# Sigmoid attention with a token and channel mixer: channel products in seven-product form, cast loads, DMA transposes and a fixed order on every engine

## Chip, cores, metric

One core of one Trainium2 chip. The metric is device time in microseconds (us), the median of several executions; a run's time is 1.7 to 1.9 us more than its own span. A run is called slow here when it is over 1.5% above the fastest of its kernel. Medians are of all runs, ratios of the fast ones alone. Engines: PE is the TensorE matmul, DVE VectorE, ACT ScalarE, POOL GpSimd, SP SyncE (which here only issues DMAs). The granted clock is the share of its full clock at which TensorE was let run. A bank is a piece of PSUM, the memory into which TensorE writes its sums.

## The reference, cut to what matters

```python
scores = q @ k.T / 8 - log(448)                  # 8 batches, 12 heads, 448 x 64
x = concat_heads(sigmoid(scores) @ v)            # [8, 448, 768]
u = x + (relu(x.T @ w_tok1) @ w_tok2).T          # token mixer, 448 -> 256 -> 448
out = u + relu(u @ w_ch1) @ w_ch2                # channel mixer, 768 -> 1536 -> 768
```

All tensors are float32; inside, products are float16 with float32 sums.

## The kernel before

Two batches form a group; there are four groups. A group has six head pairs, each with seven score tiles (`scores`), one set of value products and a turn back, then token products (`tok1`, `tok2`), turns of the sums (`uturn`) and the two channel products (`ch1`, `ch2`). The attention of group g+1 is interleaved with the products of group g, over everything but `tok1`. A visit is two score tiles, one behind the other. The order is fixed by hand on TensorE only; a scheduler arranges the other engines. Cut to what the argument touches:

```python
def turn(i):                                  # k and q turned by TensorE, 7 + 7 transposes
    for what in ("k", "q"):
        ps = bank(...)
        for j in range(J):
            nc.tensor.transpose(out=ps[:, j, :, :], in_=src[:, j, :, :], identity=ident)
        nc.vector.tensor_copy(out=kt_or_qt, in_=ps)

def ch1(cb, j0, j1):                          # first channel product, directly
    for db in range(NDB):                     # 6 matmuls into one bank
        nc.tensor.matmul(out=ps, lhsT=w_ch1_t[:, db, 128*cb:128*cb+128], rhs=uT[:, db, j0:j1, :], ...)
    nc.vector.tensor_scalar(out=h2aT[:, cb, j0:j1, :], in0=ps, scalar1=0.0, op0=MAX)

def ch2(j, half):                             # second: 12 matmuls, then one addition and a store
    ...
with tc.manual_schedule(engines={mybir.EngineType.PE}):
    for f in attention_atoms(0): f()          # first group: nothing to interleave with
    for g in range(NG):
        for f in front: f()                   # tok1
        weave(attention_atoms(g + 1), rest)   # tok2, uturn, ch1, ch2 with attention of g+1
```

## Time and profile before

| what | before |
|---|---|
| time | 438.31 us (437.31 to 440.04, 3 runs) |
| span of the profile (of an execution at a granted clock of 0.994), TensorE busy | 432.8 us, 396.2 us |
| first token product of groups 0, 1, 2, 3 starts at | 67.6, 164.8, 262.0, 359.1 us |
| one period: length, TensorE idle | 97.2, 0.8 us |

A period is the time from one group's first token product to the next group's. As TensorE idles for 0.8 us of it, work taken off TensorE ought to come out of the time as long as nothing else takes TensorE's place. The page and the windows behind this are shown in the prediction.

### The profile page before, as it was taken

How to read it: one execution, taken by the hardware profiler on the slowest of the kernel's cores; microseconds unless marked ns; L12 is line 12 of the kernel's file. 1: busy time of each engine (PE TensorE's matmuls, PEld its weight loads, DVE VectorE, ACT ScalarE, POOL GpSimd, SP SyncE). 2: the span in 40 equal slices, each digit the busy share in tenths (PEclk: the TensorE clock that was granted, in tenths of full speed). 3: DMA queues.
4: the chain of work that ended last, by engine and by line, in shares of the span. 5: the costliest groups of instructions: out<-in, count | busy, mean ns of one | idle time of the engine just before them, and what ended most of it. 6: DMA issues, size and time to landing. Idle time of an engine off the chain costs nothing.

```text
span 432.8 us, 8713 instructions
## 1 busy us (share of the span) xinstructions
PE 396.2 (92%) x3712; PEld 215.7 (50%) x3712; DVE 174.8 (40%) x312; ACT 216.8 (50%) x277; POOL 74.5 (17%) x105
## 2 busy tenths in 40 slices
PE   1775668999999999999999999999999999999995
PEld 1343335444555555444565555444555555546663
DVE  2131213845542224844542224844542224855322
ACT  1768884774546643775546643765546643300000
POOL 3851516021221211021221211011000000000000
PEclk9999989999999999999999999999999999999999
DMA  8999999335237643234337643200002221000234
GB/s 202 246 261 248 259 266 216 85 87 108 60 69 180 161 92 69 77 88 105 67 63 180 163 93 73 71 2 2 2 2 74 73 74 38 2 0 2 54 94 109
DMA packets 28023, 44.51 MB, mean 103 GB/s; under 512 B 3280, under 2 KB 23504, under 8 KB 27984
## 3 DMA queue, kind: packets, MB, share of 16 engines
q1 hardware_dynamic: 18304, 33.04, 28.6%
q0 software_dynamic: 9680, 10.92, 15.4%
q8 instruction: 29, 0.48, 0.5%
q14 instruction: 10, 0.08, 0.1%
HBM read 43.84 MB, written 11.01 MB: 127 GB/s over the span
## 4 chain that ended last, share of the span: by engine, by line
PE 85%; ACT 7%; issue 3%; DVE 2%; DMA 1%; SPq 0%; ACTq 0%; DVEq 0%
DMA rawq_0_76<-in_q_dram 1%; PE xa_5_0_787 L168 1%; PE xa_0_0_273 L168 1%; PE c_2_5_1_4890 L286 0%; PE c_2_4_1_4846 L286 0%; PE c_2_4_0_4809 L286 0%; PE c_2_3_1_4746 L286 0%; PE c_2_2_0_4654 L286 0%; PE c_2_1_1_4615 L286 0%; PE c_2_0_0_4490 L286 0%; PE c_1_6_0_3556 L286 0%; PE c_1_5_1_3507 L286 0%; PE c_1_4_1_3463 L286 0%; PE c_1_4_0_3426 L286 0%; PE c_1_3_1_3363 L286 0%
## 5 line engine op out<-in xcount | busy, mean ns | idle before, releaser
L267 PEld LDWEIGHTS <-w_ch_t 128*128 128x128 f16 x576 | 53.4, 98 | 53.8 <-issue 9.7
L286 PEld LDWEIGHTS <-h2aT_4980 128*128 128x128 f16 x168 | 16.4, 98 | 10.9
L286 PEld LDWEIGHTS <-h2aT_3597 128*128 128x128 f16 x168 | 15.6, 98 | 12.5 <-issue 3.2
L286 PEld LDWEIGHTS <-h2aT_2214 128*128 128x128 f16 x168 | 15.6, 98 | 12.5 <-issue 3.2
L286 PEld LDWEIGHTS <-h2aT_831 128*128 128x128 f16 x168 | 15.6, 98 | 12.5 <-issue 3.2
L240 PEld LDWEIGHTS <-w_tok_n 128*64 128x64 f16 x224 | 12.1, 108 | 9.0 <-issue 4.8
L222 PEld LDWEIGHTS <-w_tok_t 64*128 64x128 f16 x224 | 10.6, 94 | 7.8 <-issue 1.0
L131 PE MATMUL tk_0_165<-ident,k_0_74 128*128 128x128 f16 x7 | 0.9, 311 | 7.3 <-DVE k_0_74 L83 7.3
L154 ACT ACTIVATE attn_0_0_184<-qk_0_0_183,att_bias 128x896 f16<-128x896 f32 x1 | 1.0, 1007 | 10.1 <-PE qk_0_0_183 L147 10.1
L131 PEld LDWEIGHTS <-k_0_74 128*128 128x128 f16 x7 | 0.7, 141 | 7.3 <-DVE k_0_74 L83 7.3
L99 DVE COPY w_tok_n<-w_tok_s 128x896 f16<-128x896 f16 x1 | 1.6, 1562 | 5.5 <-DMA w_tok_s<-in_moe_w_tok_dram 5.5
L147 PEld LDWEIGHTS <-kT_0_163 64*64 64x64 f16 x28 | 1.1, 129 | 4.7 <-issue 4.5
L190 DVE COPY x_nat_162<-xb_5_820 128x896 f16<-128x896 f16 x1 | 0.6, 625 | 6.6 <-PE xb_5_820 L187 6.6
L83 DVE CAST k_0_74<-rawk_0_71 128x896 f16<-128x896 f32 x1 | 1.1, 1086 | 5.3 <-DMA rawk_0_71<-in_k_dram 5.3
L83 POOL CAST k_5_3738<-rawk_5_3735 128x896 f16<-128x896 f32 x1 | 0.9, 933 | 12.4 <-issue 12.4
L147 PEld LDWEIGHTS <-kT_2_329 64*64 64x64 f16 x28 | 0.9, 104 | 4.3 <-issue 3.5
L83 POOL CAST k_4_3725<-rawk_4_3722 128x896 f16<-128x896 f32 x1 | 0.9, 934 | 12.4 <-issue 12.4
L83 POOL CAST k_4_959<-rawk_4_956 128x896 f16<-128x896 f32 x1 | 0.9, 933 | 12.4 <-issue 12.4
L83 POOL CAST k_4_2342<-rawk_4_2339 128x896 f16<-128x896 f32 x1 | 0.9, 933 | 12.4 <-issue 12.4
L135 DVE COPY kT_1_225<-tk_1_227 128x896 f16<-128x896 f16 x1 | 0.6, 624 | 5.9 <-PE tk_1_227 L131 5.9
L147 PEld LDWEIGHTS <-kT_5_669 64*64 64x64 f16 x28 | 0.9, 106 | 4.3 <-issue 3.3
L75 POOL DMA_DIRECT2D v_3_953<-in_v_dram x2 | 1.2, 593 | 10.2 <-DMA w_ch_t<-in_moe_w_ch_dram 10.2
(1646 smaller groups left out, 1126.6 us busy)
## 6 DMA issues: line engine op xcount, KB each, us to landing
w_ch_t<-in_moe_w_ch_dram POOLq DMA_DIRECT2D x2, 2304.0 KB, 29.3
rawk_0_71<-in_k_dram SPq DMA_DIRECT2D x2, 224.0 KB, 4.0
rawq_0_76<-in_q_dram SPq DMA_DIRECT2D x2, 224.0 KB, 5.6
rawk_1_89<-in_k_dram SPq DMA_DIRECT2D x2, 224.0 KB, 7.3
rawq_1_94<-in_q_dram SPq DMA_DIRECT2D x2, 224.0 KB, 7.8
rawk_2_102<-in_k_dram SPq DMA_DIRECT2D x2, 224.0 KB, 7.1
rawq_2_107<-in_q_dram SPq DMA_DIRECT2D x2, 224.0 KB, 6.3
rawk_3_119<-in_k_dram SPq DMA_DIRECT2D x2, 224.0 KB, 7.2
```

Source lines behind the costliest of these rows:

```text
L75: eng.dma_start(out=t[64 * b : 64 * b + 64, :, :, :], in_=src[2 * g + b, 2 * i : 2 * i + 2].rearrange("h (p j) e -> p h j e", j=J),)
L83: eng.tensor_copy(out=t[:, :, :, :], in_=raw.rearrange("p h j e -> p j h e"))
L99: nc.vector.tensor_copy(out=w_tok2_n[:, :, :, :], in_=w_tok2_s.rearrange("t c (p j) -> t c j p", j=J),)
L131: nc.tensor.transpose(out=ps[:, j, :, :], in_=src[:, j, :, :], identity=ident[:, :])
L135: nc.vector.tensor_copy(out=kt[:, :, :, :], in_=ps[:, :, :, :])
L147: nc.tensor.matmul(out=ps[64 * b : 64 * b + 64, h, 0:S], lhsT=kT[i][64 * h : 64 * h + 64, j, b, :], rhs=qT[i][64 * h : 64 * h + 64, b, :, ...
L154: nc.scalar.activation(out=at[:, :, :], in_=ps[:, :, 0:S], func=SIGMOID, bias=bias_t[:, :], scale=att_scale,)
L168: nc.tensor.matmul(out=ps[b][64 * h : 64 * h + 64, :], lhsT=vf[64 * b : 64 * b + 64, h, j, :], rhs=attn[(i, j)][64 * b : 64 * b + 64, h, : ...
L222: nc.tensor.matmul(out=ps[b][:, :], lhsT=w_tok1_t[64 * b : 64 * b + 64, j, 128 * tcb : 128 * tcb + 128], rhs=x_nat[64 * b : 64 * b + 64, j ...
L240: nc.tensor.matmul(out=ps[64 * b : 64 * b + 64, :], lhsT=w_tok2_n[:, tcb, j, :], rhs=h1T[:, b, tcb, c], start=(tcb == 0), stop=(tcb == 1),)
L267: nc.tensor.matmul(out=ps[:, :, :], lhsT=w_ch1_t[:, db, 128 * cb : 128 * cb + 128], rhs=uT[:, db, j0:j1, :], start=(db == 0), stop=(db == ...
L286: nc.tensor.matmul(out=ps[:, :], lhsT=h2aT[:, cb, j, :], rhs=w_ch2_t[:, cb, c], start=(cb == 0), stop=(cb == NCB - 1),)
```

## The change

Its intent is to take work off TensorE. The seven-product form (Strassen's) cuts each matrix into four blocks and makes the product from seven products of blocks instead of eight, with sums of blocks before and after. The diff has over 900 lines; its core:

```diff
-with tc.manual_schedule(engines={mybir.EngineType.PE}):
+with tc.manual_schedule(engines=None):              # written order on every engine
-    eng = nc.gpsimd if what == "v" else nc.sync      # k, q raw on SP, rearranged and cast by POOL
+    nc.gpsimd.dma_start(out=t16, in_=src)            # k, q, v: cast loads, all on the Pool queue
 # k and q of groups 1 to 3
-    nc.tensor.transpose(...) x 14; nc.vector.tensor_copy x 2
+    nc.vector.tensor_copy(out=m, in_=raws...)        # rearranged on DVE, one buffer each
+    nc.sync.dma_start_transpose(out=t, in_=m)        # in the visit that starts the head before
 # sums of groups 1 to 3
-    nc.tensor.transpose x 6; nc.scalar.activation(COPY)
+    nc.sync.dma_start_transpose(out=uT[:, :, j], in_=u16)
 # ch1 and ch2: Strassen's seven products of half size instead of eight
+    row_sums(...)                                    # 4 DVE sums of the left matrix, per part
+    piece(1): mm(x, A1, W1); save x                  # x accumulates on: 1, then 6, 7, 4
+    piece(2): mm(y, A2, W2); out11 = clamp(y + saved)
+    piece(6): mm(x, ...); save x ... piece(7), (4), (5), (3)
+    ch2 order of a block: for p in (1, 2, 6, 5, 7, 4, 3): piece(p); add it to u (and twice where needed)
 # interleaving: attention of g+1 lies over ch1(g) and two of three ch2 blocks only;
 # then tok1(g+1), third block, tok2(g+1) with its turns, odd block of g
-    weave(attention_atoms(g + 1), rest)
+    weave(ch1 + blocks[0] + blocks[1], attention(g + 1)); tok1; blocks[2]; tok2; last
 # PSUM: scores, values and turns back share two pairs of banks
 # first group: two value steps behind each score, value copies on DVE
```

I call the stretch in which scores are interleaved with products the **woven stretch**, and what follows up to the next group's first channel product the **token part**.

## The prediction

> **What bounds the kernel now.** I read the page's busy table and slices first, then a stretch by windows, then the chain that ended last, then the timeline of one stretch.
>
> The page of the kernel before (busy us and share, then 40 slices in tenths):
>
> ```profile
> span 432.8 us, 8713 instructions
> PE 396.2 (92%) x3712; PEld 215.7 (50%) x3712; DVE 174.8 (40%) x312; ACT 216.8 (50%) x277; POOL 74.5 (17%) x105
> PE   1775668999999999999999999999999999999995
> ACT  1768884774546643775546643765546643300000
> ```
>
> PE is full from slice 8 on; only the first 70 us are not PE's. One period in the middle, by windows (PE, PEld, DVE, ACT, POOL busy, clock, DMA share):
>
> ```profile
> 167.00:264.00 97.00, 96.17 (x930) 51.92 (x928) 42.47 (x77) 53.76 (x70) 18.02 (x24) 1.00 0.43 100
> ```
>
> The token products of the four groups start at 67.6, 164.8, 262.0 and 359.1, so a period is 97.2 us, and PE is idle for 0.8 us of it. The chain of waits agrees:
>
> ```profile
> PE 85%; ACT 7%; issue 3%; DVE 2%; DMA 1%; SPq 0%; ACTq 0%; DVEq 0%
> ```
>
> The timeline gives the prices that I use:
>
> ```profile
> 83.60 1.00 ACT L154 ACTIVATE attn_0_2_1163<-qk_0_2_1162,att_bias 128x896 f16<-128x896 f32 x1
> 84.49 1.01 ACT L154 ACTIVATE attn_0_3_1170<-qk_0_3_1169,att_bias 128x896 f16<-128x896 f32 x1
> ...
> 90.51 0.36 PE L147 MATMUL qk_1_0_1257<-qT_1_1207,kT_1_1206 64*64 64x448 f16 x4
> 90.80 0.51 PE L257 MATMUL ut_6_1264<-ident,u_0_6_1152 128*128 128x128 f16 x6
> 91.15 1.46 PE L267 MATMUL c_0_4_0_1272<-uT_830,w_ch_t 128*128 128x512 f16 x6
> 92.44 1.46 PE L267 MATMUL c_0_5_0_1280<-uT_830,w_ch_t 128*128 128x512 f16 x6
> 92.65 0.69 DVE L274 TENSOR_SCALAR h2aT_831<-c_0_4_0_1272 128x512 f16<-128x512 f32 x1 [1.55 <-PE c_0_4_0_1272 L267]
> ```
>
> Sigmoids follow each other every 0.89 us although each lasts 1.0. Six matmuls of 512 take 1.29 us, 0.216 each. Four score matmuls of 64x64 run side by side and cost 0.19. Score to transpose takes 0.29, so a change of the array's tiling costs 0.1. DVE starts 0.2 us after the last matmul has been issued.
>
> **What the Trainium skill says.** "TensorE: Matmul & The Clock Gate", Back-to-back issue gap: N/2.4 + 2.5 ns. The trace agrees: 0.216 us for 512, and 1.95 us for twelve of 384, 0.1625 each; so 0.189 for 448. "TensorEngine Tiling (Array Packing)", Key Properties: a change of tiling mode drains the engine; the trace puts it at the 0.1 us above. "VectorE: DVE Perf Modes", the perf-mode tier table: a 16-bit tensor_tensor in SBUF reaches 2x, anything from PSUM in fp32 1x. The trace agrees for PSUM (692 ns for 512 elements is 533 at 0.96 GHz plus 159); it has no 16-bit sum, so I estimate 768/2/0.96 + 159 = 0.56 us. The same page, The three transpose paths, gives 1309 ns for a 128x128 transpose by DMA; the trace has no transposing DMA, and this is my least certain number.
>
> **The change, part by part, for one middle period.**
>
> PE before: k and q turns 84 x 0.056 = 4.7; scores 42 x 0.19 = 8.0; values 6 x 1.33 = 8.0; turns back 42 x 0.056 = 2.4; token products 4.6 and 4.6; sum turns 42 x 0.056 = 2.4; first channel product 12 x (6 x 0.216 + 6 x 0.163) = 27.3; second 14 x 12 x 0.163 = 27.4. Sum 89.4; the 7.8 to 97.2 are some 55 changes of tiling and the idle 0.8.
>
> PE after: seven products for eight. First channel product 7 x 6 x 3 x 0.189 = 23.8 (-3.5). Second: 7 x 3 x 6 x 0.1625 = 20.5, and the odd seventh token block directly 24 x 0.1625 = 3.9, together 24.4 (-3.0). The turns of k, q (-4.7) and of the sums (-2.4) go to the DMA queues. Sum 75.8, with some 54 changes of tiling 81.3. If PE stayed the bound a period would fall from 97.2 to about 82.
>
> DVE has to pay: 42.5 before. Added are 18 add-and-clamp operations and 6 copies of 448 (estimate 448/0.96 + 159 = 0.63 each), 23 instead of 14 additions of 384 (0.555, of which 0.09 overlaps the next), 4 x (0.56 + 0.46) sums of rows for the first product, 12 x 0.56 for the second, 12 rearrangements of k and q (about 0.5) and 6 copies of 896 from PSUM (1.09). The 24 clamps (0.69, 0.56) and the copies of turned k and q fall out. It comes to about 62 us net of overlap. ACT has 42 x 0.895 = 37.6, 8 clamps and 12 saves of 0.43. Neither exceeds 82.
>
> But the three now wait for each other. I walked the written order, which is now fixed on every engine.
> - Attention woven into the channel products: PE work 23.8 + 13.7 (two of three blocks) + 18.4 + 5.4 of tiling changes = 61.3. Scores come in twos with two PSUM pairs. Often one product piece of 0.57 lies between two visits: 0.38 + 0.2 + 0.57 = 1.15 of PE for 1.79 of ACT, a stall of 0.6, with a save on ACT 1.0. In one place two visits are adjacent (2.0). Values and turns back now take one of the same two pairs (0.4 to 0.6 each). An addition must leave PSUM before the next product accumulates there: 0.2 + 0.555 + 0.06 = 0.8 between the last two pieces of a block. Charged in full, this is 14 us, stretch 75. I take half of it, since a wait on PE lets ACT and DVE catch up: 68.
> - Token part, no attention: token product 4.7, third block 6.85 + 0.8, then DVE alone sets the pace: the trace of the last group has one token row block every 1.40 us (two additions, one cast), 9.8, plus 2.4 for sums put before the last. Then the last DMA transpose, and only then the next product. 4.7 + 7.7 + 12.7 + about 2 = 27, though PE has work for 20.
> A period: 68 + 27 = 95, hardly below 97.2. The gain of 16 us of PE work goes to waits.
>
> Start: before, the first product stage begins at 67.6. ACT ran 42 sigmoids and 12 copies in 54 us with gaps; after, the copies are DVE's and score and value steps alternate, so 12.3 + 42 x 0.895 = 50, and two more for the last values: 52. Loads: the trace took 26 MB from HBM in its first 76 us, 0.34 MB/us; what is needed by then (14.4 MB) has come by about 47, also as cast loads. That is 15 us gained. The first token part then waits for DVE: 1.6 + 5.4 for weight sums (four of 2304 elements, 1.35), 1 rearranging, 9.8 + 2.4: first channel product at about 73.5, against 83.3.
>
> End: 23.8 + 20.5 + 3.9 = 48.2 of products without attention, stalls before each block (its sums 2.4 and the first addition before the third piece, 1.8) and inside (0.8) about 8, last store 4: 60. Before: 59.5 from the first channel product.
>
> Sum: 73.5 + 3 x 95 + 2 (sums of the second weights in the first period) + 60 = 420.5. Time minus span was 5.5 before: **426**.
>
> **Rivals.**
> 1. PE stays the bound: waits overlap far better than I walked. Periods of 86: 73.5 + 258 + 2 + 58 + 5.5 = 397. For it: mean shares of ACT (about 50 of 86) and DVE (62) leave room. Against: fixed order, two score buffers.
> 2. All stalls count in full: periods of 103, time 450. For it: before, single waits for ACT in the first 60 us cost PE 1.0 each, and the stall sizes are sums of measured durations. Against: the interleaving seems chosen with care.
> 3. The transposes by DMA are the bound. Only two free buffers hold the cast sums, so the third cast waits for the first transpose; at 4 us each the token part is paced by 2.3 instead of 1.4 and gains 6 us a period; time 445 to 470. Against: 1.3 us for 128x128, and six or seven blocks of one transfer should overlap.
> 4. First loads late on the single Pool queue: 3 to 8 us once. Against: the first cast from the Pool queue (v) landed in 4.2 us before.
>
> **Range and chances.** The sum of parts is 139 + 3 periods + 5.5 within 5 us; the period is what I do not know: 86 to 104. That gives 402 to 457; I take 400 to 456. A gain over 2% needs less than 429.5, a period below 96. The walk alone would say slower, the sums of work say much faster; I lean a little to faster: 0.53, same 0.20, slower 0.27.
>
> **What would show it.** Right: token products of the groups start about 95 apart, PE busy below 85% of the span, about 325 us; first token product near 52; in the woven stretch PE waits for sigmoids and DVE additions; in the token part DVE is over 90% busy and PE under 75%. Wrong: PE above 90% busy (rival 1), waits of sums or of turned k and q for a DMA (rival 3), or a first part above 60 us (rival 4). Matmul pitches other than 0.189 and 0.1625, or an add-and-clamp far from 0.63, would break the sums themselves.

## The result, and the profile after

The kernel after took **495.3 us** (494.83 to 496.85, 4 runs) against 437.81 for the kernel before in the same rounds, a ratio of 1.1355 (95% interval 1.1283 to 1.1427). Ratios here are the mean time of one kernel's fast runs over that of the other's of the same rounds, so not quite the ratio of the medians. The prediction said 426 and gave slower a chance of 0.27.

The page of the kernel after (as before: busy us and share, then tenths in 40 slices; PEclk is the granted TensorE clock):

```profile
span 493.4 us, 7956 instructions
...
PE 386.2 (78%) x3190; PEld 188.6 (38%) x3190; DVE 288.9 (59%) x500; ACT 203.4 (41%) x256; POOL 90.2 (18%) x155
...
PE   3767776786979887488888887778888886799775
...
ACT  2798637364655300646655220445756320022000
...
PEclk9998998797999997979999997779999999799999
```

From slice 8 on, where TensorE was full before, it is 0.4 to 0.9 busy, no other engine is near full, and the clock drops to 0.7 in several slices. That is a kernel bound by waits. By stages (windows of the profile after: length, busy us of PE, PEld, DVE, ACT, POOL, granted clock, DMA share, GB/s), the second woven stretch, the token part after it, and the end:

```profile
199.14:281.48 82.34, 66.90 (x581) 30.25 (x582) 47.32 (x79) 44.43 (x54) 21.43 (x36) 0.96 0.74 99
281.48:314.14 32.66, 25.00 (x187) 14.29 (x187) 20.07 (x40) 5.39 (x10) 0.00 (x0) 0.90 0.46 94
427.91:493.40 65.49, 51.51 (x276) 26.78 (x276) 38.45 (x69) 6.52 (x12) 0.00 (x0) 1.00 0.18 49
```

| stage | predicted | measured |
|---|---|---|
| start to first token product | 52 | 58.2 |
| to the first channel product | 21.5 | 20.5 |
| woven stretches, three | 68 each, and 2 once: 206 | 87.9 + 82.3 + 81.2 = 251.5 |
| token parts, three | 27 each: 81 | 32.5 + 32.7 + 32.5 = 97.7 |
| end, from the last group's first channel product | 60 | 65.5 |
| sum | 420.5 | 493.4 |

Of the 73 us that were missed, 45.5 lie in the woven stretches, 16.7 in the token parts and 10.7 at the start and end. Where they come from can be read off the timeline. This is the start of a woven stretch in the kernel after (start, us, engine, line, operation; in brackets the idle time before it and what ended it):

```profile
201.88 1.19 POOL L106 DMA_DIRECT2D k<-in_k_dram  x2 [47.95 <-DVE pk L174]
...
202.96 1.41 SPq L178 DMA_TRANSPOSE qT<-pq  x1
...
205.09 0.38 PE L190 MATMUL qk<-qT,kT 64*64 64x448 f16 x4
...
206.86 0.61 DVE L174 COPY pk<-k 128x896 f16<-128x896 f16 x1
...
210.99 0.62 DVE L174 COPY pq<-q 128x896 f16<-128x896 f16 x1 [3.52 <-DMA qT<-pq]
211.00 0.59 PE L190 MATMUL qk<-qT,kT 64*64 64x448 f16 x4 [5.53 <-DMA qT<-pq]
...
211.52 1.30 PE L393 MATMUL x<-uT,w 128*128 128x448 f16 x3
```

The transpose of q for the second head is issued at 202.96 and its first score runs at 211.00: 8.0 us later, with TensorE idle for 5.53 of them. DVE waits for the same transpose, because the transpose still reads the only buffer of rearranged q. And the three matmuls after the wait take 1.30 us where three such took 0.74 a moment before: the clock has halved.

The first line points to what slows the transpose. The rearrangement of k frees the buffer of raw k, and POOL at once issues the load of the next group's k into it; q and v follow, and all share the DMA engines with the transposes (DMA share 1.22 from 205 to 211 us). The last four transposes of k and q in this kernel (352.63 to 364.24), with no group left to load, land in 2.9 to 3.0 us; the other 32, beside such loads, in 4.4 to 8.4. No run took the loads away alone, so that they are the cause is read from the trace, not tested.

The token part of the kernel after:

```profile
186.91 0.56 DVE L314 CAST u<-u 128x768 f16<-128x768 f32 x1 [1.69 <-DMA uT<-u]
...
187.99 0.98 PE L302 MATMUL yn<-h1T,w_tok_n 128*64 128x384 f16 x8 [2.19 <-DVE u L309]
...
191.40 6.33 PE L558 MATMUL d<-w,h2T 128*128 128x384 f16 x24 [0.41 <-DVE u L309]
...
195.78 0.56 DVE L314 CAST u<-u 128x768 f16<-128x768 f32 x1
...
199.14 0.74 PE L393 MATMUL x<-uT,w 128*128 128x448 f16 x3 [0.91 <-DMA uT<-u]
```

The third cast waits for a DMA transpose to free its buffer, TensorE waits for the cast's engine, the 24 products of the odd block then take 6.33 us (4.06 in the last group, where the clock is full), and the next product again waits for a transpose: that of the last cast, issued at 196.37 and landed at 199.09. The slow 24 products end at 197.73, before it, so they do not lengthen this part. The clock in this part, by windows (the last three numbers are the granted clock, the DMA share and GB/s):

```profile
186.00:188.00 2.00, 0.01 (x2) 0.01 (x2) 1.09 (x3) 0.00 (x0) 0.00 (x0) 1.00 0.49 78
188.00:191.40 3.40, 2.46 (x16) 1.29 (x16) 2.96 (x7) 0.00 (x0) 0.00 (x0) 0.68 0.59 116
191.40:194.50 3.10, 3.10 (x10) 1.43 (x10) 2.87 (x6) 0.00 (x0) 0.00 (x0) 0.50 0.93 82
```

It is 1.00 up to the hole of 2 us and 0.50 after it, when TensorE has work again.

### The profile page after: what moved, and what is told of

Read it like the earlier page. It is cut to its first block, busy times and chain, and to the rows that moved or that the text cites. A ratio compares the mean times of both kernels' runs of the same rounds, so it can differ in the third digit from the quotient of the medians.

```text
span 493.4 us, 7956 instructions
## 1 busy us (share of the span) xinstructions
PE 386.2 (78%) x3190; PEld 188.6 (38%) x3190; DVE 288.9 (59%) x500; ACT 203.4 (41%) x256; POOL 90.2 (18%) x155
## 5 line engine op out<-in xcount | busy, mean ns | idle before, releaser
L197 ACT ACTIVATE attn<-qk,att_bias 128x896 f16<-128x896 f32 x168 | 160.3, 1008 | 133.8 <-PE qk L190 124.4
L190 PE MATMUL qk<-qT,kT 64*64 64x448 f16 x672 | 62.1, 405 | 31.1 <-ACT attn L197 16.7
L393 PEld LDWEIGHTS <-w 128*128 128x128 f16 x504 | 45.5, 100 | 79.3 <-issue 46.1
L106 POOL DMA_DIRECT2D k<-in_k_dram x48 | 29.0, 615 | 213.2 <-DVE pk L174 199.4
L411 DVE CUSTOM_DVE_ANT_0 h2T<-z,c 128x448 f16<-128x448 f32 x48 | 30.0, 624 | 48.6 <-ACT c L406 37.0
L190 PEld LDWEIGHTS <-kT 64*64 64x64 f16 x672 | 20.4, 110 | 70.8 <-issue 68.1
L206 PE MATMUL xa<-attn,v 64*64 64x448 f16 x672 | 43.0, 377 | 0.8 <-ACT attn L197 0.8
L393 PE MATMUL x<-uT,w 128*128 128x448 f16 x144 | 37.5, 371 | 7.4 <-ACT c L406 2.5
L393 PE MATMUL x<-s,w 128*128 128x448 f16 x144 | 37.6, 372 | 7.2 <-DVE c L408 6.5
L106 POOL DMA_DIRECT2D v<-in_v_dram x48 | 28.9, 614 | 33.0 <-PE xa L206 30.6
L106 POOL DMA_DIRECT2D q<-in_q_dram x48 | 29.3, 627 | 6.9 <-DVE pq L174 5.9
L512 PEld LDWEIGHTS <-r 128*128 128x128 f16 x216 | 20.5, 98 | 20.5 <-issue 6.2
```

What stands on the lines that cost most here:

```text
L106: nc.gpsimd.dma_start(out=t[64 * b : 64 * b + 64, :, :, :], in_=src[2 * g + b, 2 * i : 2 * i + 2].rearrange("h (p j) e -> p h j e", j=J),)
L190: nc.tensor.matmul(out=ps[64 * b : 64 * b + 64, h, 0:S], lhsT=kT[(g, i)][r, j, b, :], rhs=qT[(g, i)][r, :, b, :], start=True, stop=True,)
L197: nc.scalar.activation(out=at[:, :, :], in_=ps[:, :, 0:S], func=SIGMOID, bias=bias_t[:, :], scale=att_scale)
L206: nc.tensor.matmul(out=ps[b][64 * h : 64 * h + 64, :], lhsT=vf[r, h, j, :], rhs=attn[(g, i, j)][r, h, :], start=(j == 0), stop=(j == J - 1),)
L393: nc.tensor.matmul(out=ps[:, :], lhsT=W(p, n, cb), rhs=A[p](n), start=(first and n == 0), skip_group_check=True, stop=(n == KD - 1),)
L411: nc.vector._custom_dve(dve_ops.TENSOR_ADD_SAT, out=h[:, KC * half + cb, :, b, :], in0=ps.rearrange("c (j p) -> c j p", j=J), in1=snap[(cb ...
```

## The experiments

Seventeen kernels ran. Times are medians; each ratio is against the kernel before in the same rounds, and the kernel after stands at 1.1355.

| run | time, us | ratio (95%) |
|---|---|---|
| e1 k, q turned on TensorE | 539.95 | 1.2337 (1.2245 to 1.243) |
| e2 sums turned on TensorE | 489.63 | 1.1151 (1.1078 to 1.1225) |
| e3 both | 532.0 | 1.2112 (1.2031 to 1.2193) |
| e4 direct channel products | 479.14 (fast runs 471.82, 478.69) | 1.0839 (1.0708 to 1.097) |
| e5 second turn issued earlier | 476.08 | 1.0905 (1.079 to 1.102) |
| e6 e2 + e5 + new pace | 487.66 | 1.1154 (1.1044 to 1.1265) |
| e7 e6 with direct products | 456.48 | 1.0436 (1.0294 to 1.0577) |
| e8 kernel before, written order everywhere | 455.86 | 1.0397 (1.0238 to 1.0556) |
| e9 e2 + e5 + block order | 459.15 | 1.0474 (1.0409 to 1.0539) |
| e10 e9, scores over the whole period | 462.26 | 1.0561 (1.0478 to 1.0645) |
| e11 e10 with direct products | 455.2 | 1.0392 (1.0324 to 1.046) |
| e12 kernel before with the new start | 426.98 | 0.9746 (0.9672 to 0.982) |
| e13 kernel after, order fixed on TensorE only | 490.7 | 1.1226 (1.1097 to 1.1354) |
| e14 e9, order fixed on TensorE only | 473.38 | 1.0831 (1.0739 to 1.0923) |
| e15 e12, k and q turned by DMA, early | 422.02 | 0.9656 (0.9573 to 0.9739) |
| e16 e15, first two heads on TensorE | **412.71** | 0.9442 (0.937 to 0.9513) |
| e17 e16, sums by DMA too | 429.34 | 0.98 (0.9738 to 0.9863) |

### Undoing the DMA transposes: e1, e2, e3

```diff
 # e1: in every group
-turn_by_dma(g, i + 1)        # ahead of the visit's scores
+turn_by_pe(g, i + 1, "k"); turn_by_pe(g, i + 1, "q")   # behind them, through bank m3
 # e2: in every group
-uturn_dma(g + 1, j)
+if j >= 2: uturn_pe(g + 1, j - 2)                      # as the kernel after does for group 0
-if j == 5: ch1_sums(g + 1, 0, 4)                       # four row sums ahead of the last sum
+if j == 6: ch1_sums(g + 1, 0, 4)                       # behind it
```

In e1 the turn had to go behind the visit's scores: ahead of them, the copy into the buffer of k waits for a score that stands behind it on TensorE, and the simulator reports a deadlock.

> The kernel after, with k and q of every group turned on TensorE (84 turns a period, through the bank of the second piece) in place of DMA transposes; the sums still go by DMA. Theory A (what was lost beyond my walk is lost to DMA transposes that land late and to the half clock after the waits): the woven stretch loses its wait for qT (3.6, 5.5 and 3.4 us in the three periods) and the slow matmuls behind it (about 2 us), and pays 4.7 + 1.2 us for turns: within 5 us of 495, say 488 to 498, with a granted clock near 0.97. Theory B (the fixed order with two pairs of score banks is what stalls; transposes are incidental): turns and their copies on DVE add 6 to 8 us a period, time 512 or more.

> The kernel after, with the sums of all groups turned on TensorE and copied by ACT, as the kernel after does for its first group; k and q still by DMA. Theory A: the token part falls from 33.4 us to about 26 (no third-cast wait of 2.2 twice, the odd block's 24 products in 3.9 instead of 6.3 because the clock stays up, no wait of 1.5 for the last transpose), time 470 to 478. Theory B: token part 31 or more, because DVE sets its pace; time above 488.

> Both of the former: no transposing DMA at all. Theory A: the gains add up, 464 to 478, granted clock above 0.97. Theory B: 500 or more. If e1 and e2 are both small and this one is large, the shared SP queue couples them.

e2 came out between its theories: its time is above the 488 of theory B, its token parts are below that theory's 31. They fell from 32.5, 32.7, 32.5 to 30.5, 29.2 and 29.1 at a granted clock of 1.00, 9 us in all, 6 in the time. But e2 holds two edits: it also puts four row sums (2.3 us of DVE) behind the last sum. How much belongs to the transposes isn't shown; the casts' waits for them in the kernel after, gone in e2, are 6.3 us over the three groups. e1 and e3 fell into theory B's open ranges (512 or more, 500 or more), but for a reason of their own. Waits of e1 (engine, line, what it waited for, us, times, longest):

```profile
PE tk L164 <- DVE pk L160: 27.2, 11, 5.6
PE tq L164 <- DVE pq L160: 26.6, 24, 1.2
```

I had built a bad test: each turn on TensorE now stands directly behind its own rearrangement on DVE in the fixed order, so TensorE waits out a round trip in 35 of the 48. It says nothing about the transposes by DMA; it shows what an unskewed dependence costs under fixed order. e3 has the same fault.

### Only the place of one transpose: e5

```diff
 # attention_atoms(g), visit at the start of head i
-if i + 1 < NP: turn_by_dma(g, i + 1)
+if 0 < i and i + 1 < NP: turn_by_dma(g, i + 1)
 # main loop, ahead of tok1(g + 1)
+turn_by_dma(g + 2, 1)        # for group 1: inside its token part
```

> The kernel after, with only the place of one transfer changed: the second turn of k and q of groups 1 to 3 is issued in the token part before, not in the first visit of the woven stretch, seven scores ahead of its use. Same transposes, same queue, same number. Theory A' (a transpose takes 5 to 8 us from issue, and this one is asked for too late; the wait also halves the clock for 3 us): the wait for qT goes (12.6 us in all) and with it some 2 to 3 us of slow matmuls per stretch: woven stretches of 74 to 76 instead of 81 to 88, time 470 to 477. If the waits for qT only move to the third turn, or the DMA queue is at its limit: above 486.

As expected, with 476.08 us. The waits for qT are gone from the list, the woven stretches are 80.4, 75.7 and 75.2 instead of 87.9, 82.3 and 81.2, and the clock in the second is 0.98. The pair of transposes now stands 7 us further ahead of the stretch in the first group and 33 us in the other two; it takes even longer there (qT 9.8 and 10.7 us), but nobody waits. Its windows, second stretch and token part:

```profile
191.59:267.27 75.68, 66.32 (x580) 30.14 (x580) 46.04 (x77) 43.19 (x52) 17.85 (x30) 0.98 0.67 91
267.27:299.97 32.70, 25.13 (x187) 14.35 (x187) 21.38 (x42) 5.39 (x10) 3.56 (x6) 0.90 0.82 130
```

So 19 us of the time come from where one pair of transfers per group stands, the number of transfers being the same. With it the loads that the rearrangement releases moved too: six of POOL's pieces, 3.56 us, now lie in the token part. The second stretch now has the length that I had walked with every stall in full, 75.

### Direct products in the kernel after: e4

```diff
-return [(0.57, piece(p, cb)) for p, cb in chain_order(KC)]            # 42 pieces of 3 matmuls
+return [(1.14, plain(cb, b)) for cb in range(NCB) for b in range(2)]   # 24 of 6, one clamp each
-order.append([(0.98, piece(p, n)) for p in (1, 2, 6, 5, 7, 4, 3)])
+order.append([(1.95, direct(half, j)) for j in (2*n, 2*n+1) for half in range(2)])
```

> The kernel after with both channel products done directly (six and twelve accumulating matmuls, 448 and 384 wide), no sums of rows or weights, no saves; loads, DMA transposes, written order and interleaving stay. PE works 6.5 us more a period, DVE and ACT much less. Theory A: the product form isn't what lost the time, so the time stays or rises, 490 to 515. Theory C (the additions, saves and sums that Strassen's form puts between PE, DVE and ACT are the loss): below 470.

Between the theories: 479.14 us, or 475.3 by its two fast runs, 20 us faster than the kernel after (495.3) with 6.5 us more of products in each period. The windows are of its fastest run, 471.82. Second stretch, token part and end:

```profile
184.99:268.63 83.64, 69.88 (x612) 33.67 (x612) 35.31 (x55) 39.75 (x42) 21.43 (x36) 0.98 0.81 102
268.63:296.47 27.84, 23.20 (x194) 13.05 (x193) 15.26 (x30) 4.74 (x10) 0.26 (x1) 1.00 0.43 93
410.20:470.10 59.90, 54.70 (x312) 30.43 (x312) 22.77 (x38) 0.00 (x0) 0.00 (x0) 0.98 0.21 53
```

The woven stretches (80.5, 83.6 and 85.9) sum to 250 us, as in the kernel after with its 251.5: the 5.5 us of TensorE work that the seven products save in each are eaten there by waits. Token part (27.8 against 32.7) and end (59.9 against 65.5) are shorter with more work. At the end, where no attention disturbs, the direct form idles for 59.9 - 54.7 = 5.2 us, most of it the last store; the seven-product form has 48.2 us of products in 65.5. Its waits stand in the timeline of the kernel after, two in every block:

```profile
460.04 1.14 PE L512 MATMUL x<-w,r 128*128 128x384 f16 x6 [1.48 <-DVE u L523]
...
463.77 1.14 PE L512 MATMUL x<-w,h2T 128*128 128x384 f16 x6 [0.65 <-DVE u L523]
```

The first is the third piece waiting for an addition behind four row sums on DVE (each 0.56 us), the second is piece 4 waiting for the addition of piece 7 out of the same bank.

### Pace and block order: e6, e7, e9

```diff
 # e6: sums on TensorE (e2), early turn (e5), and
-atoms.append((0.6, visit)); values 2.0; back 0.6
+atoms.append((1.8, visit)); values 0.5; back 0.2
 # e9: e2 + e5 at the old pace, and
-for p in (1, 2, 6, 5, 7, 4, 3)
+for p in (1, 2, 6, 5, 7, 3, 4)      # x y x z x z x: no two neighbours on one bank
+if p == 7: three of the four row sums of block n + 1
```

> Three edits at once: sums turned on TensorE (e2), the early second turn (e5), and the weights of the interleaving set so that visits of two scores lie about evenly (visit 1.8, values 0.5, turn back 0.2 instead of 0.6, 2.0, 0.6), since two visits 1.4 us apart can't be served by ACT at 1.79 for two sigmoids. Expected: waits of PE for sigmoids in a woven stretch from 6.3 to about 2.5 us; 489 - 21 (early turn) - 10 (pace) = 458, 450 to 466. If the lockstep of PE with DVE and ACT is spread over so many small waits that each removed one comes back elsewhere: 470 or more.

> The same three edits, with channel products direct instead of in seven products. If Strassen's form costs its gain in waits for additions, saves and sums, this one is as fast as e6 or faster (445 to 460); if those waits matter little once the transposes and the pace are mended, e6 is faster by about the 26 us of PE work saved, less 8 for the waits of sums in the last group: e7 at 470 or more.

> Sums turned on TensorE (e2) and early second turn (e5), the original weights of the interleaving, and in the second product's blocks the pieces in the order 1 2 6 5 7 3 4 instead of 1 2 6 5 7 4 3, so that no two neighbours share a bank, with three of the next block's four row sums put behind piece 7. In the last group these waits were 0.65 in each block and 1.4 to 1.5 at each block's third piece, 6.2 us in all; they should fall below 2. Expected: 476 - 6 (sums) - 4.5 (end) - 3 x 1.5 (blocks of the periods) = 461, 456 to 468. If the lockstep moves the waits elsewhere: above 468.

e6 was 30 us slower than expected. The waits for sigmoids did fall (from 19.8 us in e5 to 7.5), but another took their place:

```profile
PE qk L190 <- DVE xT L223: 24.4, 15, 6.1
```

The scores after a set of values need the pair of banks that DVE still has to copy the values out of, and in the fixed order that copy stands behind sums and saves. The old pace left room behind the values; the new one took it. e7 met its range, but as e6 was spoilt by the pace, the two say less about the product form than e10 and e11 do.

e9 hit: 459.15 against 461 expected. Its second stretch and token part:

```profile
189.14:263.33 74.19, 64.88 (x584) 30.14 (x582) 46.44 (x80) 44.97 (x54) 17.84 (x30) 1.00 0.68 94
263.33:292.72 29.39, 25.70 (x230) 15.01 (x229) 20.65 (x41) 9.27 (x16) 3.56 (x6) 1.00 0.60 94
```

The end fell to 61.6 us. Between e5 (476) and e9 lie 17 us; 6 of them are e2's, so the block order is worth about 11, if the two add up.

### Where the scores lie: e10, e11

```diff
-weave(ch1 + blocks[0] + blocks[1], attention(g + 1)); tok1; blocks[2]; tok2; last
+weave(blocks[2] of g - 1 + tok2 + uturn + last + ch1 + blocks[0] + blocks[1], attention(g + 1)); tok1
```

> As e9, and the scores of the next group laid over the whole period (also over the token part and the third block) as the kernel before does, not over the first product and two blocks alone. PE work of a period is 78 us and tiling changes 6 to 7. If the loss of Strassen's form is that ACT and DVE are asked for too much in one part of the period and stand idle in the other: periods of about 92 instead of 105, time 420 to 435. If it lies in each single dependence of piece, save and addition: periods of 100 or more, 445 or more.

> As e10 with channel products direct (no saves, no row sums). PE work 85 us a period and 6 to 7 of tiling, few waits: periods of 96 to 98, time 428 to 442. Against e10 it gives the worth of the seven-product form once the rest is mended: e10 faster by 8 us or more if the form pays, slower if its waits eat it.

e10 came out as its second theory said, e11 missed its range. With the scores over the whole period e10's second and third periods are 103.0 and 104.7 us, e9's were 103.7 and 105.0. But the test isn't clean: waits for sigmoids fell from 20.4 us in e9 to 10.7, while each of these two periods got a wait for qT, 3.3 and 3.5 us, that e9 didn't have. Less those, the periods would be 99.7 and 101.2 (an estimate), some 4 us below e9's and far from the 92 expected: crowding of ACT into one part explains at most a part of the loss. e11, direct, has 99.4 and 102.2: again no longer with 6.5 us more of products. In all, 15.0 us (e10) and 14.4 us (e11) of waits for qT came back; 8.2 and 12.5 of them fall in the first period, whose first scores now come soon after the loads. Less those, e11 would be at 441 (455.2 - 14.4), near the kernel before; that is an estimate which takes waits as simply additive.

### The fixed order: e8, e13, e14

```diff
 # e8, in the kernel before
-tc.manual_schedule(engines={mybir.EngineType.PE})
+tc.manual_schedule(engines=None)
 # e13 in the kernel after, e14 in e9: the reverse
```

> The kernel before with the written order on every engine instead of on TensorE alone, nothing else. If the fixed order as such costs (no engine may pass over a waiting instruction): 450 or more. If it only binds together with the other edits: 433 to 445, same as before.

> The kernel after with the written order fixed on TensorE alone, as in the kernel before, and nothing else: TensorE's rows are the same, the other engines' are arranged by the scheduler, which puts rearrangements of k and q earlier. If the fixed order on the other engines is what makes the transposes late and DVE blocked: below 480, waits for qT gone. If the waits come from the dependences of the pieces and the two pairs of banks, which the order of TensorE already sets: 485 to 500.

> As e9 (sums turned on TensorE, early second turn, pieces of a block so that no neighbours share a bank) with the written order on TensorE alone. What is left of the loss in e9 is some 20 us of waits for sigmoids, 44 of them. If those come from the two pairs of banks and TensorE's own order, which stay: 452 to 465. If the fixed order of ACT and DVE holds sigmoids up behind saves and copies: below 448.

Fixing the order of the kernel before costs it 4%: its loads of the next group stand right ahead of their stretch in the text, where the scheduler had moved them up; POOL, which rearranges k, waits 150 us for its raw loads in e8. But freeing the order of the kernel after gains 1% (1.1226 against 1.1355, intervals that overlap), and of e9 loses 3%. e13, its first part and its second stretch:

```profile
0.00:83.26 83.26, 40.17 (x462) 21.44 (x464) 37.26 (x57) 40.75 (x43) 42.55 (x75) 0.79 1.10 163
210.92:290.06 79.14, 67.07 (x581) 30.24 (x582) 47.65 (x82) 43.18 (x52) 21.41 (x36) 0.97 0.62 100
```

The first part grows from 58.2 to 83.3 us, since the scheduler puts work that waits ahead of copies that TensorE needs: DVE stands still for 6.8 us before the weight sums (for their load), and later for 12.7 and 5.9 us before rearrangements of k and q of group 1 (for a load and for a transpose). Behind the last two stands the copy of values for which TensorE waits 15.7 us. What follows is 30 us shorter (periods of 97.5, 109.3 and 106.9 us instead of 108.5, 114.8 and 113.9), in part because the scheduler also moves the rearrangements of k and q up, which e5 does by hand. Where that is done already, in e9, freeing the order loses 23.6 us at the start and gains only 10.5 later (e14). So the fixed order in the kernel after saves at its start about what it costs later, and isn't the loss by itself. e14 has waits of 22.5 us for sigmoids, e9 of 20.4: these stay when ACT and DVE are free, so I take them to come from what stays, TensorE's own order and the two pairs of banks.

### Parts of the change on the kernel before: e12, e15, e16, e17

```diff
 # e12: attention_atoms(0) written as in the kernel after
+two value steps behind each score; value copies on DVE
 # e15: e12, and for g >= 1
-turn(i): 14 nc.tensor.transpose, 2 copies, just ahead of head i
+nc.sync.dma_start_transpose(kT / qT), one whole head earlier
 # e16: heads 0 and 1 of group 1 back on TensorE
 # e17: e16, and uturn(j) by dma_start_transpose in all groups
```

> The kernel before with one part of the change alone: in the first group, which has no product to interleave with, two value steps behind each score and the copies of the values on DVE instead of ACT. The first token products then start at 58 to 60 as after instead of 67.6, and the periods stay 97: 428 to 432, if the loads (raw, not cast, on two queues) keep up; 438 if they don't.

> The start of e12 (first group with value steps behind each score) on the kernel before, and k and q of groups 1 to 3 turned by DMA, each issued a whole head (some 15 us) ahead of its first score, with the channel products, the interleaving and the free order of the kernel before. TensorE is the bound there, so what is taken off it should come out of the time: 84 turns and 12 changes of tiling, 5.9 us a period: 427 - 17 = 410, 405 to 417. If transposes by DMA cost more than they take off wherever they stand: 425 or more.

> As e15, but the first two heads of group 1 are turned on TensorE as before, because their loads come while the DMA queues are still full: in e15 the first qT of group 1 came 10.8 us late and the clock fell behind it, so its first period was 104 us beside 91.7 for the others. Expected: first period about 93.5, time 422 - 10 = 412, 408 to 416. If the wait was for the loads themselves, not for the transposes: 418 or more.

> As e16, and the sums of all groups turned by DMA too, in the free order and interleaving of the kernel before, where scores lie between a sum and its first product and four buffers hold the cast sums. If it is the place that makes a transpose by DMA dear, as in the token part of the kernel after: 42 turns and their changes of tiling come off TensorE, 3 us a period, time 399 to 406 less what the last group, with no scores to cover, waits (2 to 4 us): about 404. If sums by DMA cost wherever they stand: 412 or more.

e12: its first token product starts at 57.1 instead of 67.6, and 426.98 us is 1 us below the expected 428 to 432. e15 has later periods of 91.74 us instead of 97.2, 5.5 off where 5.9 were expected, but its first period is 104.3, with one wait of 10.8 us for the first qT, so that 422.02 missed the expected 405 to 417. e16 takes that wait away and comes to 412.71 us, 5.6% faster than the kernel before, with periods of 95.1, 91.7 and 91.7. Its DMA issues (size where there is one, and median us to landing):

```profile
kT<-k SPq DMA_TRANSPOSE x16, 3.0
qT<-q SPq DMA_TRANSPOSE x16, 3.0
```

The same transposes, the same size, from the same queue; in the kernel after, those of k and q land 2.9 to 8.4 us after issue (median 5.6). In e16 most have no load beside them; the few beside loads or stores take up to 5.2. e17 missed by 25 us: sums by DMA cost there too, 11 us in the first period, 1.2 in each of the next two and 3.6 at the end. The first is a matter of the queue: the first sum is cast at 65.4, but its transpose is issued at 77.19, as the SP queue first has to issue loads of k and q that wait for POOL; the first product then waits 12.3 us. The later waits in e17:

```profile
PE c L326 <- DVE u L309: 5.6, 3, 2.0
```

The tool puts these waits down to the cast of a later sum. But in all three the fourth transpose, on which the first product depends, lands within 0.1 us of that cast's end (in the second group at 178.39, the cast ends at 178.45, the product starts at 178.44), so the trace doesn't tell the two apart. A sum is needed a few microseconds after it is made; k and q are known a period ahead. I take this to be why one pays by DMA and the other doesn't; the runs show that it is so, not that this is the reason, and 11 of the 16.6 us that e17 loses against e16 are the queue's in the first period.

## Why the prediction was wrong, point by point

- **Prices right.** Pieces of three 448-wide matmuls follow each other at 0.57 us (0.189 each) and of six 384-wide ones at 0.98 (0.1625), the add-and-clamp took 0.624 us (0.63 predicted), the row sums 0.56, the copy of values 1.09. (In "VectorE: DVE Perf Modes", the perf-mode tier table has 1x from PSUM for tensor_tensor only, and up to 2x for copies; the 0.624 and 1.09 us of 448 and 896 elements fit 1x.)
- **Saving of TensorE's work right, its use wrong.** The gain was put into a sum that lets other engines cover it; e4 and e11 show that in this structure the direct form with more work is faster. TensorE's busy time was to be 325 us and reads 386: mine is a sum of pitches; I put the difference down to the profile, which counts the 0.16 us tail of each group (0.73 beside 0.57) when a wait follows, and to the clock, which averaged 0.941. How much each makes isn't shown.
- **The step that failed most: "I take half of it, since a wait on PE lets ACT and DVE catch up: 68."** With the late transpose mended, the stretch measures 75.7 and 75.2 (e5), 74.2 and 75.6 (e9): the walk in full, 75, was right, and the half was a guess against my own working. That is 7 us a period, 21 in all. The stalls too are near the walk's 14: in e5's second stretch TensorE is idle for 9.4 us, and the tails of 0.16 us ahead of some 20 waits, which count as busy, add 3.2 (an estimate). Rival 2, all stalls in full, was right in this term; e9's periods are 102 to 105, its 103.
- **A wait that no step had:** the turn of q, issued seven scores ahead of its use. I took turns to the DMA queue as free but for the last sums; waits for turned k and q stood among the signs of being wrong, but had no time in the sum. They are 12.6 us in the kernel after (3.6, 5.5 and 3.4). In all the place of this turn cost 20.3 us of woven stretches (251.5 to 231.2 in e5) with the half clock behind it. With the last two points, 41 of the 45.5 us are told; in the first stretch a wait of 4.0 us for DVE, busy with the weight sums, is 2 more than I had put in.
- **Token part, 27 against 32.5.** Its three pieces measure alike in all three groups: 14.0 us to the second token product (4.7 + 7.7 = 12.4 in the walk), 15.8 from there to the end of the last cast (12.7), 2.8 to the next product (2). Rival 3 was right in kind: in each group two casts wait for a transpose to free their buffer, 2.1 us, and the last transpose takes the 2.8; it was wrong in size, with 6 us. The odd block's products were rightly counted as lying beside DVE's work: even at half clock, 6.3 us, they end before the last transpose lands. DVE was to be over 90% busy there and was 20.07 of 32.66; TensorE, to be under 75%, was 25.00.
- **Start, 58.2 against 52.** The first sigmoid starts at 10.1, earlier than the 12.3 that I took over. But the 42 sigmoids then take 45.8 us, not 37.6: ACT waits for scores in 11 gaps, 5.9 us in all. On TensorE in this part waits for copies that turns back need are 5.4 us, which I had not charged. Loads were no trouble: it stays below the 60 of rival 4, and e12 shows the new start worth 11 us.
- **End, 65.5 against 60.** 8 us of stalls and 4 of last store were charged; the products of 48.2 leave 17, of which 5 are the last store and 12 stalls.
- **Slips in the sums.** The 5.5 us from span to time compare the median with the profile of a faster execution; a run is 1.7 to 1.9 us above its own span. 9.8 + 2.4 is 12.2 and was entered as 12.7; the first token part's terms give 72.2 and were entered as 73.5. They are small beside the 73 us.

The runs show where the 73 us lie, and that moving one turn, turning the sums on TensorE and reordering the blocks take 36 us off (e9); the rest is argued from waits. What stays open: whether the seven-product form would pay in the kernel of e16, whose free order and four rotating banks it doesn't fit as written; and e9's remaining 20 us against the kernel before. Its list shows 20.4 us of waits for sigmoids, 44 of them, but no run removed them without new waits in their place. The product form alone isn't it either: e7 and e11, direct, stand at 1.04.

## What to carry to other kernels

Work taken off a bound engine is only won if no dependence takes its place: count each new hand-over between engines in full, above all under a fixed order, and don't discount a walk by a hope. A transpose by DMA is cheap where its input is known long ahead and dear in a chain whose result is needed at once; moving the issue of one pair per group ahead by 7 to 33 us was worth 19 us here. Before a buffer is freed earlier, ask what its release will start and what that will share. A large change that loses may hold parts that win: two of them, tried on the kernel before, gave 412.71 us.

## What the Trainium skill lacked or had wrong

- "VectorE: DVE Perf Modes", The three transpose paths, gives 1309 ns for one 128x128 block by DMA. No page says what a transfer of seven blocks takes from issue to landing: here 3.0 us (median of e16); in the kernel after 2.9 to 3.0 without loads beside it and 4.4 to 8.4 with them; up to 18.5 in e15 while the first loads filled the queues. In the kernel after each also holds its issuing queue for 1.22 to 1.46 us.
- "Advanced Engine Details and Errata", X-Bar Transpose (TRN2), expects 350 to 400 GB/s. A transfer of 128 x 896 x 2 bytes in 3.0 us is 76 GB/s, latency included. For a single transfer of this size the measurement decides; no run here kept transposes coming without a break, so the page's bandwidth itself isn't tested.
- "TensorE: Matmul & The Clock Gate", HAM oscillation — how this bites in real kernels, states the rule as no idle gaps above some 3.4 us. In the token part of the kernel after the longest gap was 2.19 us, with four of 0.4 to 0.5 around it, and the granted clock still fell from 1.00 to 0.50 at 189.21, for 6.8 us. (A second HAM failure mode, on the same page, tells of short idles that come often, without a figure for them.)
